# A layered kernel whose order is written out by hand: three constant products less, the modulation's first loads earlier, and all instructions listed anew

## The chip, the core and the metric

The kernel runs on one core of one Trainium2 chip. The core has a matrix engine (TensorE, PE in the profile, with its weight loads as PEld), a vector engine (VectorE, DVE), a scalar engine (ScalarE, ACT), a general one (GpSimd, POOL), and SyncE (SP), which here issues nearly all DMAs. Each engine works through its own instructions in order and waits on semaphores for the others. The metric is the device time of one execution in microseconds (us); lower is better. A time is the median of several runs.

## What is computed

Two token-mixing layers with adaptive normalisation, all in float32, on x of 2048 rows by 512 columns. The modulation vectors come from one row c:

```python
    x = A_x
    mod = (_silu(c) @ w_mod).reshape(c.shape[0], 6, 1, -1)
    sa, ca, ga, sb, cb, gb = (mod[:, 0], mod[:, 1], mod[:, 2], mod[:, 3], mod[:, 4], mod[:, 5])
    h = _layernorm(x, axis=-1) * (1 + ca) + sa
    x = x + ga * _A_ref(h, A_wqkv, A_w_phi, A_wo)
    h = _layernorm(x, axis=-1) * (1 + cb) + sb
    x = x + gb * _B_ref(h, B_w1, B_w2, B_w3, B_w4)
    return x
```

A is a linear attention with a learned feature map: there are 32 heads of 16 columns; keys and queries go through a small matrix per head, `w_phi`, and two softmaxes, and the sums go through wo. B is layernorm, w1, gelu, shifts along the rows and w2, then layernorm, w3, gelu and w4, with both halves added to their input; w1 and w2 are 512 by 512, w3 is 512 by 1376 and w4 is 1376 by 512.

## The kernel before

**Stages.** The rows are worked in 16 tiles of 128, two tiles making a chunk (8 chunks). First the per-head matrices are folded into the key and query weights on TensorE (`load_folded`, line 648: eight products of a loaded tile `rk` with a block-diagonal matrix `bd` that is made from a small constant and a mask). Then every chunk is normalised, turned by TensorE transposes, scaled and shifted by the modulation's columns (`h_chunk`, 685), and multiplied to keys, values and queries (`k_feat` 736, `q_feat` 764); the keys' features are summed with the values into one accumulator. Queries go to DRAM. The second stage (`phase_a`, 909) takes them back chunk by chunk, makes attention's output, wo, the second modulated norm, w1 and the shifts with w2. The last stage multiplies by w3 and w4 with a Strassen-like scheme of seven products for eight. The large weights and activations are split in a high part and a remainder (`hi_lo`), and three fast products of the parts stand for one product in full precision (`three`).

**The start.** `body` loads c and the identity from ScalarE's queue (`load_act`) and a small constant from SyncE's, fills a matrix `ones` on GpSimd, and issues nine constant products of `ones` with itself (lines 500 to 502), whose result nobody reads; each is four matmuls of 128 by 128 in float32, and each such matmul runs as two passes, so it makes eight records in the profile. `mod_cols` (529) makes the columns of sa and 1 + ca: silu of c (exp on ScalarE, then add, reciprocal and product on VectorE), a broadcast of it to `wide`, four loads `mod2` of 0.5 MB each, four groups of products of `wide` with them, a copy of the result out of PSUM, two transposes on TensorE and two small copies. The other four modulation vectors are made in full rows later, from sixteen more loads (`mod_acc`).

**What sets the order.** The program builds a list of operations first (class `Plan`, 283), numbers them as they are made, and then issues them in the order that the string `ORDER` gives (line 40, read in `order`, 352). A number may carry a letter that moves the operation to another engine it can run on (A for ScalarE, V for VectorE, G for GpSimd). Nothing else orders the work: one engine's queue is the subsequence of `ORDER` that falls to it. `SLOT` gives each tile the buffer it lies in, one character per tile; a tile whose buffer was in use waits for the last reader of the tile before. In SyncE's queue of before, the loads come in this order: four tiles of x, with the small constant after the second; two tiles `rk`; the four `mod2`; two `rk`; a tile of x; then the other four `rk` with a tile of x among them; then wv, x and the modulation's further loads. TensorE's queue begins with the nine constant products, one folded-weight product, four transposes of the first chunk, the four groups of modulation products, then more transposes (the third chunk's among them) and the other seven folded-weight products. ScalarE's queue begins with c's load, then a pass over a tile of x of the third chunk, and the identity's load behind that.

The mask and constant that make `bd` run on VectorE and GpSimd (`make_bd`, 641). Two layer norms are in use: one with its statistics on VectorE (`layernorm`, 572: the first chunk) and one on ScalarE (`layernorm2`, 612).

Of the kernel before, what the change touches and what calls it, by code (L numbers as in the profile page):

```python
# [164 lines left out]
)  # L165
SLOT = {
    "pp": "354206170301136260517505607442523070157475601660106031401453313745662015634523405103645651314210"
          "4326265450622670302462",
    "bd": "c3",
    "w": "124657de12834c6d075e18",  # L170
    "rk": "9768efjh",
# [1216 lines left out]
```

## Time and profile before

| | |
|---|---|
| median of 3 runs | 556.39 us (556.19 to 556.42) |
| the profiled execution | 556.38 us |
| its span, first to last instruction | 554.6 us |
| granted TensorE clock | 0.999 |
| DMA, mean over the span | 225 GB/s |
| moved by DMA | 124.90 MB |

How to read the rows of the profile: a line of the timeline has a start and a duration in us, the engine, the line of the code, the instruction, what it writes and reads by the program's names, and a count where several were merged; in brackets stands the idle time before it and who ended it. All matmuls have line 471, since one helper issues them, so groups are told apart by their names: `pp<-const` are the constant products, `pp<-mod,const` the modulation's, `pp<-bd,rk` the folded weights', `pp<-w,hh` keys, values and queries, `pp<-w,oT` wo, `pa<-nT,w` w1. A line of the windows has a stretch, its length, then per engine the busy time and the count, then the granted clock, the DMA's share and its GB/s. A line of the waits has who waited, for whom, the sum, how many times, and the longest.

### The profile page before, as it was taken

The page shows a single profiled execution, that of the slowest core. Times are in us where ns is not written, and L with a number is a line of the kernel's source. Part 1 is how long each engine was busy: PE and PEld are TensorE (multiplying, and loading weights), DVE is VectorE, ACT ScalarE, POOL GpSimd, SP SyncE. Part 2 cuts the span into 40 slices and gives each one's busy share as a digit, 9 for nine tenths or more (in the row PEclk, how much of TensorE's full clock was granted, in tenths as well). Part 3 has the DMA queues.
Part 4 walks back from the last instruction along what each step waited for, and adds up shares of the span by engine and source line. Part 5 has one row for each costly group of instructions (what it writes and reads, how often), then busy time and mean ns, then how long its engine had stood idle before and what let it go on. Part 6 is the DMA issues. An engine that isn't in the chain of part 4 may idle for free.

```text
span 554.6 us, 12399 instructions
## 1 busy us (share of the span) xinstructions
PE 548.3 (99%) x4522; PEld 491.5 (89%) x4522; DVE 484.6 (87%) x901; ACT 352.1 (63%) x833; POOL 339.5 (61%) x348
## 2 busy tenths in 40 slices
PE   9999999999999999999999999999999999999997
PEld 8888788888777788888889999999999999999996
DVE  3899997999999999999898788788788777888876
ACT  4789988644344788978888786867352535235540
POOL 3289849788799999986986533516334453133522
PEclk9999999999999999999999999999999999999999
DMA  8964651654765668687898888896976796572212
GB/s 317 386 215 148 212 161 42 214 173 143 247 193 158 221 212 232 238 294 256 269 298 267 274 297 276 281 324 250 382 232 241 264 379 204 174 249 93 59 58 76
DMA packets 63749, 124.90 MB, mean 225 GB/s; under 512 B 7140, under 2 KB 26852, under 8 KB 59592
## 3 DMA queue, kind: packets, MB, share of 16 engines
q1 hardware_dynamic: 63400, 124.04, 67.3%
q8 instruction: 35, 0.57, 0.4%
q14 instruction: 26, 0.21, 0.1%
q10 hardware_dynamic: 288, 0.07, 0.1%
HBM read 89.74 MB, written 34.35 MB: 224 GB/s over the span
## 4 chain that ended last, share of the span: by engine, by line
PE 61%; DVE 1%; DVEq 0%; issue 0%
PE pa L471 26%; PE ac L471 20%; PE pp L471 14%; PE pt L480 1%; DVE pT L762 0%; DVE pp L437 0%; DVE xb L418 0%; DVEq L1384 0%; DVEq L418 0%; DVEq L762 0%
## 5 line engine op out<-in xcount | busy, mean ns | idle before, releaser
L471 PE MATMUL pp<-w,hh 128*128 128x512 f32 x576 | 137.9, 396 | 0.0
L471 PEld LDWEIGHTS pp<-w,hh 128*128 128x128 f32 x576 | 106.8, 188 | 25.6 <-ACT qe L401 0.8
L471 PE MATMUL pa<-bH,wq 128*128 128x256 f32 x840 | 107.7, 281 | 0.0
L471 PE MATMUL ac<-w,gg 128*128 128x256 f32 x840 | 107.2, 281 | 0.0
L471 PEld LDWEIGHTS ac<-w,gg 128*128 128x128 f32 x840 | 103.6, 188 | 1.2
L471 PEld LDWEIGHTS pa<-bH,wq 128*128 128x128 f32 x840 | 103.7, 189 | 1.0
L471 PE MATMUL pp<-w,sh 128*128 128x512 f32 x192 | 50.1, 399 | 0.0
L471 PE MATMUL pa<-nT,w 128*128 128x256 f32 x384 | 47.8, 282 | 0.9 <-DVE nT L418 0.6
L471 PEld LDWEIGHTS pa<-nT,w 128*128 128x128 f32 x384 | 46.5, 188 | 2.4 <-DVE nT L418 1.1
L471 PE MATMUL pp<-w,oT 128*128 128x512 f32 x192 | 47.7, 396 | 0.0
L471 PEld LDWEIGHTS pp<-w,oT 128*128 128x128 f32 x192 | 35.5, 188 | 8.1 <-DVE oT L418 0.4
L420 POOL TENSOR_TENSOR gg<-cu,gg 128x128 fp32r<-128x128 f32 (+1 forms) x29 | 19.0, 667 | 38.1 <-PE ac L471 18.4
L471 PEld LDWEIGHTS pp<-w,sh 128*128 128x128 f32 x192 | 34.5, 188 | 7.7 <-issue 1.0
L401 ACT ACTIVATE cu<-pa 128x512 f32<-128x512 f32 (+1 forms) x39 | 20.1, 519 | 27.5 <-PE pa L471 21.3
L588 POOL TENSOR_TENSOR rs<-mv,const 128x2 f32<-128x2 f32 x31 | 22.6, 732 | 24.3 <-ACT mv L595 23.0
L401 ACT ACTIVATE gg<-cu 128x256 fp32r<-128x256 f32 (+1 forms) x64 | 21.2, 357 | 23.7 <-PE ac L471 17.4
L420 POOL TENSOR_TENSOR e<-e,q 128x1024 f32<-128x1024 f32 x16 | 31.2, 1966 | 1.2 <-DVE q L418 1.1
L420 POOL TENSOR_TENSOR ez<-e,const 128x1024 f32<-128x1024 f32 x12 | 29.8, 2490 | 2.8 <-ACT const L401 2.8
L401 ACT ACTIVATE gg<-sg 128x512 fp32r<-128x512 f32 x37 | 22.5, 623 | 13.5 <-POOL sg L420 8.2
L418 DVE TENSOR_TENSOR gg<-sg,gg 128x512 fp32r<-128x512 f32 x38 | 26.8, 707 | 4.6 <-ACT gg L401 3.3
L401 ACT ACTIVATE cu<-cu 128x512 f32<-128x512 f32 (+1 forms) x36 | 19.3, 550 | 12.0 <-DVE cu L418 12.0
L418 DVE TENSOR_TENSOR cu<-pa,cu 128x512 f32<-128x512 f32 (+1 forms) x36 | 21.1, 593 | 6.4 <-PE pa L471 5.3
(214 smaller groups left out, 1212.4 us busy)
## 6 DMA issues: line engine op xcount, KB each, us to landing
wq<-dram SPq DMA_DIRECT2D x32, 1024.0 KB, 6.8
dram<-ws SPq DMA_DIRECT2D x35, 256.0 KB, 3.0
xl<-in_x SPq DMA_DIRECT2D x32, 256.0 KB, 4.3
dram<-qe SPq DMA_DIRECT2D x16, 512.0 KB, 2.9
e<-dram SPq DMA_DIRECT2D x64, 128.0 KB, 3.6
raw<-in_w SPq DMA_DIRECT2D x18, 256.0 KB, 3.9
mod<-in_wmod SPq DMA_DIRECT2D x16, 256.0 KB, 5.3
dram<-xl SPq DMA_DIRECT2D x16, 256.0 KB, 3.4
```

Of the source, the lines that this page charges most:

```text
L401: nc.scalar.activation(o(), i(), func, **kw)
L418: dve = ("DVE", 71 + 1.04 * o.n + 90 * (isps(a) and isps(b)), lambda: nc.vector.tensor_tensor(o(), a(), b(), op=op))
L420: pool = ("Pool", cost, lambda: nc.gpsimd.tensor_tensor(o(), a(), b(), op=op))
L471: nc.tensor.matmul(o(), a(), b(), start=s, stop=e, **kw)
L480: nc.tensor.transpose(o(), i(), ident())
L588: plan.op("Pool", 540 + 10 * m, lambda: nc.gpsimd.tensor_tensor(r(), v(), mhalf[:, :m](), op=OP.pow), [r], [v, mhalf])
```

## The change

Three things change. The constant products are six in place of nine; all operations made after them have numbers lower by three. `ORDER` is written anew in full, and `SLOT` with it. And a few operations go to other engines: counted by the letters and the engines that operations have without one, 340 of the 2801 operations that both kernels share run on another engine than before (103 from GpSimd to VectorE, 101 from VectorE to GpSimd, 58 from VectorE to ScalarE, 53 back, 16 from ScalarE to GpSimd, 9 back). What each operation computes stays.

```diff
 ORDER = (
-    "0 3 45 12 38 2 240 10 46 7 47 48 87 13 49 242 239 30 26 53 57 55 39 59 34 40 1 41 4 22 241 42 43 6 50 243 "
+    "1 10 3 42 0 4 35 2 50 54 5 52 56 23 36 31 9 11 88 85G 43 27 37 44 12 86 45 8 19 18 13 14 15 49G 38 39 51 100 "
+    "6 46 40 16G 7 41V 237 17 47 53 87 48G 55 57 62 58V 92 236 59 24 96 60 84 61 63V 67 81 25 32 68V 64 679 69 89 "
...
 SLOT = {
...
-    "rk": "9768efjh",
+    "rk": "72634eg9",
-    "xl": "10di5208hfgb4cf0ea0c4kd9f3ihj36146gb9b9508ikhj73",
+    "xl": "10ikfbdb9h23j8l640adjlk9g876e46lfdil3j080678278h",
...
     plan.at("warm")
-    for _ in range(9):
+    for _ in range(6):
         p = T("pp", [P, NK, P])
         mms([(p[:, k, :], ones, ones, True, True) for k in range(NK)], [p], [ones])
```

Read back from the two strings, the queues begin like this after the change.

- SyncE: two tiles of x, the small constant, the four `mod2` (first, third, second, fourth), six tiles `rk`, a tile of x of the third chunk, `rk`, the other such tile, `rk`, then wv's first tile, the second chunk's x and so on.
- TensorE: four constant products, the first group of modulation products, the other two constant products, the three further groups of modulation products, four transposes of the first chunk, the two transposes of the modulation's columns, a folded-weight product, the other four transposes of the first chunk, the seven other folded-weight products, then two key products and a query product of the first chunk, the second chunk's transposes, a query product, the third chunk's transposes.
- ScalarE: the identity's load, c's load, the exp of silu, then copies of the folded weights and of the first chunk; the third chunk's norm after these.
- VectorE: both first statistics, silu's steps with masks among them, a norm of the first chunk, then the modulation's copies and the split of the first chunk and of the folded weights.
- GpSimd: `ones`, a mask, the broadcast to `wide` (on ScalarE before), the first two reciprocal roots.

More of the change, by code (lines that the diff above doesn't have):

```diff
@@ L40 @@
 ORDER = (
[124 rows of a table removed]
[124 rows of a table added]
 )
 SLOT = {
[L167 to L170, printed above, removed]
-    "rk": "9768efjh",
-    "xl": "10di5208hfgb4cf0ea0c4kd9f3ihj36146gb9b9508ikhj73",
-    "st": "40d3i38fc51di08ac4jah174d1ga5f06d",
-    "mv": "51fa026ig6bf351di08i8dg27dei6e59b",
-    "rs": "62gb497302ag46bf35236be1i703938ai",
-    "nm": "78eh9cj51badh4ej897chej297ghe69cj29c08bgbf45fhjach42j17g",
@@ L177 @@
-    "xn": "gbaba47ai968db2j",
-    "mod": "l6l76g452h91di45e2",
+    "pp": "015632614340517032150643012526242367251411661166312763426267553575313027152161025567307111272635"
+          "0055072172642262056",
+    "bd": "85",
+    "w": "125634cd180254b6d83c72",
+    "rk": "72634eg9",
+    "xl": "10ikfbdb9h23j8l640adjlk9g876e46lfdil3j080678278h",
+    "st": "01b8h659g68cf15bdj7928gdc6g92if59",
+    "mv": "23fa07aej79eh68cf18f6bh7gbie5123a",
+    "rs": "54gd18ci13agj79eh2305a13e4jfb07ce",
+    "nm": "67ci9ej23b4dfh025b4di023a4gi05cd73ci06ahaeh14j894jd68bgh",
@@ L179 @@
+    "xn": "ac6e20j076ibfkic",
+    "mod": "dja8441l7ei4agf6ga",
     "mod2": "0213",
-    "kva": "2",
+    "kva": "0",
     "za": "6",
-    "hh": "0839abc0",
-    "pt": "25327461613743570652324305736521",
-    "raw": "c21k18h7715djgf362a0fhae27gf",
-    "k1": "1045013501501501",
-    "ke": "5489712089712354",
-    "k2": "5234231243234323",
-    "vv": "a7dk85gac5hbb21h",
-    "qe": "6720487161942819",
-    "q1": "2330454052043312",
-    "qt": "kkbhb78bg11b",
-    "acc": "j3lcg",
-    "kvs": "2",
@@ L194 @@
-    "pz": "7",
-    "q2": "03123513",
-    "e": "0983705304169074",
-    "ez": "2320522197506115",
-    "q3": "1245045014204250",
-    "q5": "15504152",
-    "pT": "4528179545810889",
-    "oT": "6a6ca009",
-    "nT": "b0766b9a",
-    "n": "g7dh24k4bj74g816",
-    "h": "5j7ge851ckdij4c5",
-    "gf": "27586896",
-    "sh": "95b9ae91",
-    "pa": "641235350522652635114703427320411671025643770736145372603453",
-    "wr": "35632",
-    "ws": "l6d9h3a4820k5c8chb8h2d2k7920b8f8c3d",
-    "gb": "l",
-    "tw": "54235",
@@ L212 @@
-    "bL": "17827583",
-    "nb": "979h32306d3ae5k9",
-    "yt": "3dg52b83k86hjehh",
-    "bH": "06946142097189309001918205215851",
-    "tr": "b3bj5235i0j1e29j",
-    "wq": "075e2ab923b9a23ba9b32ba932ba23ab9a32",
-    "cu": "910bdi843kjc02akf9bhe35j061ig2h41eg8b7cj",
-    "gl": "h48h9962",
-    "ac": "16455436740134572306167215764032",
-    "gg": "73961754365316475286104928316462703941562370961249647091642708964235190243756189",
-    "sg": "kec291637e7die18bdch9cakf7g3cdi602di3cj4",
-    "xb": "fg6g5d74b8fakf59",
@@ L224 @@
-    "xc": "6a134j6g8h22dh30",
-    "uu": "a3ee5c1d",
+    "hh": "0789abe7",
+    "pt": "72547173634774753001231627404702",
+    "raw": "9c3h5d79b2kfiche513a9hifgjl2",
+    "k1": "0114230103143431",
+    "ke": "4529730459817324",
+    "k2": "0451352502052531",
+    "vv": "h0ec840g7d05bh2b",
+    "qe": "7601181576971729",
+    "q1": "3252402454123154",
+    "qt": "2c30khikc02k",
+    "acc": "5kf1a",
+    "kvs": "2",
+    "pz": "4",
+    "q2": "03125315",
+    "e": "0953845341605891",
+    "ez": "3622216688880646",
@@ new lines @@
+    "q3": "1245043014204230",
+    "q5": "00032504",
+    "pT": "7466688584766450",
+    "oT": "96b3a9a6",
+    "nT": "a94baace",
+    "n": "6hh66h6hl5861454",
+    "h": "cia4ej0ckg72de3c",
+    "gf": "29470579",
+    "sh": "7e67edc7",
+    "pa": "371003132710576017436532106014275314360517374703257106341757",
+    "wr": "82032",
+    "ws": "d231ghe76gjgk921dff1b2haci9k6k1k55l",
+    "gb": "b",
+    "tw": "79265",
+    "bL": "81374028",
+    "nb": "895d50a15424dg12",
+    "yt": "7fd13408i9df3723",
@@ L226 @@
+    "bH": "64478207159823612653094704091721",
+    "tr": "k96hada5ikcl1hkl",
+    "wq": "739391ae09ae109e109ae091ea010e1a09e1",
+    "cu": "a10ki95f8j0jh81a6e4kk2l9d4g06ecj3f51k80l",
+    "gl": "lifhc6dj",
+    "ac": "45722570314275103624062315204736",
+    "gg": "95426980426801459802938176385986135927068341579637175369405638749056132790864257",
+    "sg": "hee3ae4ddlg325dd07ic8h71hik879h7d29l7h42",
+    "xb": "6cc7g43jf5gei0a9",
+    "xc": "g4lg29lh522ihglc",
+    "uu": "li7al636",
 }
```

245 rows, old and new, of the table ORDER are left out of this document.

## The prediction

> **What bounds the kernel now.** I read the page first: the engines' totals, then the chain that ended last.
>
> ```profile
> span 554.6 us, 12399 instructions
> PE 548.3 (99%) x4522; PEld 491.5 (89%) x4522; DVE 484.6 (87%) x901; ACT 352.1 (63%) x833; POOL 339.5 (61%) x348
> PE 61%; DVE 1%; DVEq 0%; issue 0%
> ```
>
> TensorE is busy for 548.3 of 554.6 us, and the chain is almost all matmuls from 211 us to the end. So the time is TensorE's work, plus what it loses at the start, at stalls, and after its last matmul. The profiled execution took 556.38 us, 1.8 us more than its span; the median of the three runs is 556.39, so sums made against this profile need no shift. The rows below are TensorE's own timeline at the start, then pieces of it cut out by two narrower windows, then the end.
>
> ```profile
> 0.98 11.09 PE L471 MATMUL pp<-const 128*128 128x128 f32 x72 [0.98 <-POOL const L498]
> 11.90 1.06 PE L471 MATMUL pp<-bd,rk 128*128 128x128 f32 x8
> 13.56 1.93 PE L471 MATMUL pp<-mod,const 128*32 128x256 f32 x32
> 15.43 1.09 PE L480 MATMUL pt<-const,xn 128*128 128x128 f32 x8
> 17.02 6.42 PE L471 MATMUL pp<-bd,rk 128*128 128x128 f32 x56
> 23.19 5.86 PE L471 MATMUL pp<-w,hh 128*128 128x512 f32 x24
> 0.98 5.70 PE L471 MATMUL pp<-const 128*128 128x128 f32 x25 [0.98 <-POOL const L498]
> 6.99 4.85 PE L471 MATMUL pp<-const 128*128 128x128 f32 x42
> 550.22 0.52 PE L471 MATMUL ac<-w,gg 128*128 128x256 f32 x3
> 550.85 0.75 DVE L418 TENSOR_TENSOR xb<-xb,ac 128x256 f32<-128x256 f32 x2 [0.86 <-PE ac L471]
> ```
>
> The nine constant products are the 72 records of the first row (4 matmuls of two passes each). They come at two rates: 25 in 5.70 us, one per 0.213 us, and from about 6.7 us on 42 in 4.85 us, one per 0.112. Real work starts at 11.90 and then TensorE hardly stops. After that start its waits on other engines are these three, 1.2 us in all, where the first chunks' normalised tiles (nT, n) are awaited, between 186 and 206 us:
>
> ```profile
> PE pa L471 <- DVE nT L418: 0.6, 2, 0.3
> PE pt L480 <- ACT n L401: 0.3, 1, 0.3
> PE pa L471 <- ACT nT L401: 0.3, 1, 0.3
> ```
>
> The second reading is VectorE's, by stages (busy time, then counts):
>
> ```profile
> 0.00:23.19 23.19, 12.54 (x34) 1.00 0.95 345
> 23.19:80.00 56.81, 55.38 (x79) 1.00 0.61 196
> 80.00:100.00 20.00, 16.92 (x26) 1.00 0.31 104
> 100.00:190.25 90.25, 88.00 (x127) 1.00 0.63 195
> ```
>
> And all engines' further on (PE, PEld, DVE, ACT, POOL, each busy time and count):
>
> ```profile
> 190.25:260.00 69.75, 69.08 (x639) 59.26 (x640) 67.99 (x118) 57.57 (x136) 60.45 (x57) 1.00 0.73 236
> 260.00:354.00 94.00, 94.00 (x733) 84.98 (x732) 80.64 (x149) 74.82 (x187) 57.94 (x69) 1.00 0.83 278
> 354.00:550.85 196.85, 196.74 (x1616) 194.30 (x1614) 162.39 (x373) 92.69 (x224) 72.47 (x111) 1.00 0.64 219
> ```
>
> 190.25 us is where the first w1 products start. From 23 us to there VectorE is busy for 160 of 167 us: it is a second limit just behind TensorE, and only its early work has room.
>
> **The constant products.** Three products of 8 records go. The 25 slow records stay, because the four products still at the head hold 32; what goes is 24 records at 0.112 = **2.7 us**. They are on the path: TensorE is busy from 0.98 on. But they also covered the wait for the first loads, so the question is what is late next.
>
> **The loads.** SyncE issues in order. Before, the modulation's four loads of half a megabyte stand behind four tiles of x, the small constants and two of the folded weights; now they stand behind two tiles of x and the constants. Rates and landings:
>
> ```profile
> 0.00:3.00 3.00, 2.02 (x9) 2.03 (x10) 0.00 (x0) 1.28 (x1) 0.39 (x5) 1.00 0.33 100
> 3.00:6.00 3.00, 3.00 (x16) 3.00 (x15) 2.20 (x8) 0.00 (x0) 0.57 (x1) 1.00 1.03 346
> 6.00:9.00 3.00, 3.00 (x26) 3.00 (x25) 0.61 (x4) 2.62 (x8) 1.76 (x3) 1.00 1.04 372
> 9.00:12.00 3.00, 3.00 (x29) 3.00 (x28) 1.63 (x7) 2.22 (x8) 1.60 (x3) 1.00 1.02 398
> 3.99 2.65 SPq L448 DMA_DIRECT2D mod<-in_wmod x4
> mod<-in_wmod SPq DMA_DIRECT2D x1, 512.0 KB, 5.8
> mod<-in_wmod SPq DMA_DIRECT2D x1, 512.0 KB, 7.5
> ```
>
> The last column of the windows is GB/s, so 0.30 MB had moved by 3 us, 1.34 by 6, 2.45 by 9, 3.65 by 12. The first modulation load landed at 3.99 + 5.8 = 9.8; with all ahead of it, it is byte 2.23 million, moved by 8.4: 1.4 us from the last byte to the landing. The third (issued 4.94, 7.5) gives the same 1.4. The queue is never empty, so the new order goes by bytes. The first load ends at 1.25 MB (the identity, now issued first on ScalarE at 0.72 in place of 6.32, is in it): moved by 5.7, landed 7.1. The third (needed second) ends at 2.29 MB: landed 9.95. The last ends at 2.82 MB: landed **11.3**, where before it was the byte 3.80 million, about 13.8. The folded weights' tiles follow, one per 0.7 us from 11.9; TensorE takes one per 0.9 us from 12.7, so they hide. What is moved back behind them, the two tiles of x for the third chunk and ScalarE's work on them, is next needed at 32 us; it hides too.
>
> **The silu of c.** The modulation's stationary operand needs c through exp, add, reciprocal, product, and a broadcast. Before it was ready at 12.0, because ScalarE had its work behind a wait for x. These rows price it:
>
> ```profile
> 3.56 0.69 DVE L574 BATCH_NORM_STATS2 st<-xl 128x6 f32<-128x512 f32 x1 [3.56 <-DMA xl<-in_x]
> const<-in_c ACTq DMA_DIRECT2D x1, 2.0 KB, 3.0
> 6.32 0.63 ACT L401 ACTIVATE xn<-xl 128x512 f32<-128x512 f32 x1 [3.87 <-DMA xl<-in_x]
> 9.58 0.19 ACT L401 ACTIVATE const<-const 128x4 f32<-128x4 f32 x1
> 10.29 0.17 DVE L445 RECIPROCAL const<-const 128x4 f32<-128x4 f32 x1
> 11.72 0.29 ACT L401 ACTIVATE const<-const 128x128 f32<-128x128 f32 x1
> 12.71 0.45 POOL L420 TENSOR_TENSOR bd<-const 128x128 f32<-128x128 f32 x1
> ```
>
> Now c's load goes second on ScalarE, about 0.4 later, and lands at 4.1 with nothing of x ahead of it. VectorE does two statistics first (the second tile of x, one tile's 0.26 MB behind the first at the rate of the 3 to 6 us row, lands at about 4.4; then 2 x 0.69), five small ones at 0.15 to 0.2 and two masks at 0.25 among them: the product is done at about 7.3. The broadcast goes to GpSimd, of which no such row exists: at least ScalarE's 0.29, at most the mask's 0.45. I take 0.4: ready at 7.7. Both ends differ by 0.2 us.
>
> **TensorE's new start, step by step.** Four constant products end at 7.4. First modulation product at 7.7 (idle 0.3), 1.93/4 = 0.45 long with its gap. Two constant products, 16 x 0.112 = 1.8, to 9.95, as the next load lands. Two modulation products to 10.85. The last load lands at 11.3 (idle 0.45); product to 11.75, drained 11.9. Four transposes of x fit behind it. Then the queue holds two transposes of the evicted sums in front of everything: they need VectorE's eviction,
>
> ```profile
> 15.57 0.42 DVE L410 TENSOR_SCALAR mod<-pp 128x256 f32<-128x256 f32 x1 [1.16 <-PE pp L471]
> ```
>
> so they start at 11.9 + 0.1 + 0.42 + 0.1 = 12.5 (idle 0.3) and end at 12.7. Eight folded-weight products (64 x 0.112 = 7.2) and four transposes (0.45) follow without a wait: the first key product starts at **20.3**. Before it started at 23.19, with 0.9 us of the third chunk's transposes (two groups of four) already done that now come later: 22.3. The lead is **2.0 us**, of the 2.7; the other 0.7 went into the new waits.
>
> [...]
>
> **Behind it, up to 30 us.** VectorE has 38 instructions listed ahead of the first key reduction, 14 of them 512 wide at 0.6 to 0.69 us, by rows about 15 us; it can start the bulk of them when the columns are there, at 13.3 (12.7 and an eviction) where the row below has 17.05, and the reduction can't start before 23.2.
>
> ```profile
> 17.05 1.59 DVE L410 TENSOR_SCALAR pt<-pt,const 128x256 f32<-128x256 f32 x3
> ```
>
> So it arrives with 15 us done where before it had 12.54 by then. The next tight place is the second chunk's first transposes at 20.3 + 8.5 = 28.8 (three products, 5.86/2 each less the overlap): one of their tiles is now normalised on VectorE, behind the second key product's first reduction, at 28.6 to 29.5. I count 0.2 us. SyncE's later loads wait for buffers as before.
>
> **The order anew.** 340 of 2801 instructions change engines, but the work of each engine stays within 3 us (VectorE +1, ScalarE -2, GpSimd +3, at the durations of before's groups). TensorE's list keeps its shape: ahead of the first w1 products stands the same work less the constants, and between the first chunk's output projection and its transposes the same filler (two num groups, two query products, three quarter projections). So the stalls there remain. VectorE's list ahead of those products trades 28 instructions (15.1 us) for 31 (17.8; 1.59/3 for the 256 wide, 0.6 to 0.69 for the 512, 1.2 for the 1024): 172.85 + 2.7 = 175.6 us. Its idle time before was 10.65 us up to 23.19, and 6.75 after. With 2.5 less at the start (15 done for 12.54): 8.1. Were the later 6.75 unchanged, the products would start at 175.6 + 8.1 + 6.75 = 190.4; without the 3.1 of 80 to 100 us, when VectorE had run ahead and waited for TensorE, at 187.3. TensorE itself gets there at 190.25 - 2.0 + 0.2 = 188.5. I take 188.7. From 354 us on VectorE has 34 us of room. The last group is the same: final matmuls, two additions of 0.4 us, two stores. Cost nothing; what would cost is the broadcast addition on GpSimd just ahead, done 0.8 us early by my count.
>
> **Sum:** -2.7 + 0.7 + 0.2 + 0.2 = **-1.6 us: 554.8**.
>
> **Rivals.**
> *The stalls go too.* VectorE reaches 190 us ahead of TensorE (187.3), so part of the 1.2 us of stalls and some switching loss vanishes: 553.8 down to 552.4. Against it: the wait for nT is a chain of transpose, copy and difference behind one quarter projection, the same in both lists.
> *VectorE takes it back.* If its idle time after 23 us is what it was, the first w1 products start at 190.4 and the end stays: 556.4, between 555.3 and 557.5. For it speaks that 2.7 us were added to its list; against it, that the 3.1 us were waiting for TensorE.
> *Slower, by VectorE's queue.* The same place: each us beyond counts fully, because behind 190 us TensorE has no idle time to give. It decides at 7.8 us of idle time after 23 us (start at 191.5, 1.2 us late); at 10, VectorE having waited for ScalarE and GpSimd inside its own order, it is 193.7 and 559.8. Nothing in the lists shows such waits, but an order anew has them somewhere.
> *Slower, cold.* If the modulation's loads landed as late as before (13.8), TensorE would sit idle from 10.85, 3 us in place of 0.45, which turns the 1.6 us gained into 0.9 lost: 557.3, or, if the slow rate came back for 5.7 us as in the row of 25, 2.7 more: 560.0. The bytes speak against it. [...]
>
> **How the numbers follow.** The forecast (553.8 to 555.3) has 0.46, the stalls' rival 0.14, VectorE taking it back 0.20, slower by its queue 0.13, cold 0.07. About 0.2%, 1.1 us, is what a measurement here can tell from no change: faster 0.60, same 0.20, slower 0.20. The range leaves out the ends of both sides: 552.4 to 558.4.
>
> **What would show it.** Right: 48 constant records, the first four modulation products between 7.7 and 12, key products from 20.3; TensorE waiting three times under half a us; w1's first products near 188.7; the end 3.8 us after the last matmul. Wrong: a wait above 1 us in the first 13 us (loads or silu), a TensorE wait at 29 us for the second chunk's tile, a first w1 product after 190, or new stalls in the last stage, for which I have no row.

## The result, and the profile after

The changed kernel takes **558.45 us** (median of 6 runs, 557.63 to 559.66) against 556.28 us (6 runs) of the kernel before: ratio 1.0036, 95% interval 1.0024 to 1.0049. It is slower, by 2 us, where I forecast 1.6 us faster. Beside the last experiments it was timed once more: 557.96 us in 12 runs, ratio 1.0027 (1.0014 to 1.0040). The profiled execution took 557.92 us with a span of 556.1, 1.5 us more than before's 554.6. The page has these lines for it: the span, the engines' totals, the chain by engine.

```profile
span 556.1 us, 12353 instructions
PE 545.4 (98%) x4498; PEld 488.6 (88%) x4498; DVE 487.7 (88%) x898; ACT 350.1 (63%) x831; POOL 345.1 (62%) x353
PE 86%; DVE 7%; DMA 3%; POOL 2%; issue 1%; DVEq 0%; ACT 0%; POOLq 0%
```

TensorE is busy 2.9 us less than before (545.4 against 548.3), near the 2.7 us of the forecast, and yet the span is longer. The chain tells where to look: VectorE holds 7% of it, where it held 1%.

TensorE's own waits, in the changed kernel (who, on what, total, times, longest):

```profile
PE pp L471 <- ACT kvs L401: 1.5, 1, 1.5
PE pp L471 <- DMA mod<-in_wmod: 1.4, 3, 1.0
PE pp L471 <- DVE pT L762: 1.1, 1, 1.1
```

The first and the last are new and long: a wait for `kvs` (the copy of the keys' and values' sums) and one for `pT` (a transposed tile of the first query group). Before, neither product waited at all. First the start, from TensorE's timeline of the changed kernel:

```profile
0.97 5.72 PE L471 MATMUL pp<-const 128*128 128x128 f32 x32 [0.97 <-POOL const L498]
7.70 0.64 PE L471 MATMUL pp<-mod,const 128*32 128x256 f32 x8 [1.01 <-DMA mod<-in_wmod]
...
10.54 1.07 PE L471 MATMUL pp<-mod,const 128*32 128x256 f32 x16 [0.23 <-DMA mod<-in_wmod]
...
20.79 8.53 PE L471 MATMUL pp<-w,hh 128*128 128x512 f32 x36
```

The start does what was forecast: first modulation product at 7.70, key products from 20.79 (forecast 20.3). Now the same two products in both timelines, the changed kernel first, then the kernel before. A row is a run of merged matmuls: a query product, which covers the time until `kvs` is copied, then the product with `kvs` (group kvb), behind another query product the one with `pT` (group num0).

```profile
154.57 3.04 PE L471 MATMUL pp<-w,hh 128*128 128x512 f32 x12
159.09 0.66 PE L471 MATMUL pp<-const,kvs 128*64 128x128 f32 x8 [1.48 <-ACT kvs L401]
...
163.86 1.16 PE L471 MATMUL pp<-pT,const 64*32 64x128 f32 x64 [1.14 <-DVE pT L762]
```

```profile
156.21 3.05 PE L471 MATMUL pp<-w,hh 128*128 128x512 f32 x12
159.19 0.67 PE L471 MATMUL pp<-const,kvs 128*64 128x128 f32 x8
...
162.76 1.16 PE L471 MATMUL pp<-pT,const 64*32 64x128 f32 x64
```

At the query product ahead of kvb the changed kernel is 156.21 - 154.57 = **1.64 us ahead**, which is the whole forecast gain. Nine microseconds later it is 163.86 - 162.76 = **1.10 us behind**: 1.48 + 1.14 us of waits. So this loss is made in one place. What stood still there shows in the queues behind the two waits; VectorE first, then GpSimd, then ScalarE, all of the changed kernel:

```profile
140.93 1.85 DVE L418 TENSOR_TENSOR ke<-ke,k 128x1024 f32<-128x1024 f32 x1
142.70 1.21 DVE L418 TENSOR_TENSOR qe<-qt,q 128x1024 f32<-128x1024 f32 x1
143.83 0.68 DVE L418 TENSOR_TENSOR w<-raw,w 128x512 fp32r<-128x512 f32 x1
144.74 1.23 DVE L418 TENSOR_TENSOR ez<-e,const 128x1024 f32<-128x1024 f32 x1 [0.23 <-ACT const L401]
145.88 2.63 DVE L418 TENSOR_TENSOR ws<-ws 128x256 fp32r<-128x256 f32 x1
148.43 1.78 DVE L418 TENSOR_TENSOR w<-raw,w 128x512 fp32r<-128x512 f32 x1
...
153.66 1.27 DVE L442 TENSOR_REDUCE q<-qt 128x32 f32<-128x512 f32 x2
```

```profile
139.28 2.41 POOL L420 TENSOR_TENSOR za<-za,ke 128x1024 f32<-128x1024 f32 x1
145.78 2.45 POOL L420 TENSOR_TENSOR ez<-e,const 128x1024 f32<-128x1024 f32 x1 [4.09 <-ACT qe L401]
148.19 1.47 POOL L420 TENSOR_TENSOR w<-raw,w 128x512 fp32r<-128x512 f32 x1
155.07 2.03 POOL L420 TENSOR_TENSOR qe<-qt,q 128x1024 f32<-128x1024 f32 x1 [5.41 <-DVE pz L437]
```

```profile
157.13 1.15 ACT L401 ACTIVATE qe<-qe 128x512 f32<-128x512 f32 x2 [5.15 <-POOL qe L420]
...
158.66 0.37 ACT L401 ACTIVATE kvs<-kva 128x256 f32<-128x256 f32 x1
```

Compare like with like on VectorE. The operation on `w` takes 0.68 at 143.83 and 1.78 at 148.43; the one on 1024 columns takes 1.21 at 142.70 and 1.85 at 140.93; the 256 wide one on `ws` takes 2.63, where the group of its kind has a median of 0.415:

```profile
L418 DVE TENSOR_TENSOR ws<-ws x9: 408/415/2628, 77.8 to 315.9; 128x256 fp32r<-128x256 f32 x9
```

That is 1.10 + 0.64 + 2.21 = 3.95 us. Each of the three begins while GpSimd runs an operation and ends only after it: `ws` at 148.51, GpSimd's `ez` at 145.78 + 2.45 = 148.23. Such time counts as busy here (2.63 us in the row of `ws`), so VectorE looks full. All of these operations, on both engines, read two tiles from SBUF. And the delay travels by the queues. The reductions of query group q8 (of q0 to q15) end at 154.9 (153.66 + 1.27); GpSimd, idle for 5.41 us, subtracts their result (`qe`) until 157.10; ScalarE's two exponentials and a `qt` stand behind that and ahead of `kvs`, which is copied at 158.66, though TensorE had gone on from `kva`'s sums to the query product at 154.57.

### The profile page after: what moved, and what is told of

Same layout as the page of the kernel before. It is cut to its first block, busy times and chain, and to the rows that moved or that the text cites. A ratio compares the mean times of both kernels' runs of the same rounds, so it can differ in the third digit from the quotient of the medians.

```text
span 556.1 us, 12353 instructions
## 1 busy us (share of the span) xinstructions
PE 545.4 (98%) x4498; PEld 488.6 (88%) x4498; DVE 487.7 (88%) x898; ACT 350.1 (63%) x831; POOL 345.1 (62%) x353
## 4 chain that ended last, share of the span: by engine, by line
PE 86%; DVE 7%; DMA 3%; POOL 2%; issue 1%; DVEq 0%; ACT 0%; POOLq 0%
PE pp L471 36%; PE pa L471 27%; PE ac L471 20%; PE pt L480 2%; DVE pz L442 1%; DMA mod<-in_wmod 1%; DVE q L442 1%; PE kva L471 1%; POOL qe L420 1%; DVE pT L762 1%; DMA wr<-in_w 1%; POOL e L420 1%; DMA const<-in_id 1%; DVE ws L418 0%; DVE ez L418 0%
## 5 line engine op out<-in xcount | busy, mean ns | idle before, releaser
L420 POOL TENSOR_TENSOR gg<-cu,gg 128x128 fp32r<-128x128 f32 (+1 forms) x28 | 17.5, 633 | 36.4 <-PE ac L471 11.3
L401 ACT ACTIVATE gg<-cu 128x128 fp32r<-128x128 f32 (+1 forms) x64 | 21.3, 354 | 18.7 <-PE ac L471 11.0
L420 POOL TENSOR_TENSOR w<-raw,w 128x512 fp32r<-128x512 f32 (+3 forms) x16 | 19.6, 1229 | 20.5 <-DVE w L410 12.0
L418 DVE TENSOR_TENSOR gg<-sg,gg 128x512 fp32r<-128x512 f32 x36 | 25.3, 706 | 7.8 <-PE pa L471 3.9
L420 POOL TENSOR_TENSOR ke<-ke,k 128x1024 f32<-128x1024 f32 x14 | 27.1, 1942 | 0.0
```

The source lines that it names most:

```text
L401: nc.scalar.activation(o(), i(), func, **kw)
L418: dve = ("DVE", 71 + 1.04 * o.n + 90 * (isps(a) and isps(b)), lambda: nc.vector.tensor_tensor(o(), a(), b(), op=op))
L420: pool = ("Pool", cost, lambda: nc.gpsimd.tensor_tensor(o(), a(), b(), op=op))
```

## The experiments

Three theories. **Turns**: VectorE's two-input operations stand still while GpSimd runs one, in turns, and the queues carry that to kvb and num0. **Length**: VectorE simply has more work listed ahead of num0. In both lists each operation taken at its median, that is about 160.6 us against 154.0 up to the transposition that num0 waits for, 6.6 us more (the expectations say 5); the forecast had looked further down, at w1's first products, and found 2.7. **Place of kvs**: `kvs` stands behind the exponentials in ScalarE's queue, and that alone is the loss. The rivals of the start are tried as well. Numbers in `ORDER` are the changed kernel's: 784 is the operation on `ws`, 672 the remainder on `w.11` (a subtraction; the expectations call it a product), 708 and 706 the two `ez`, 709 the reduction of the first, 460 the last q8 reduction, 680 `kvs`, 669 GpSimd's remainder.

**e1: the operations spread.** Three words of VectorE's list are moved, nothing else.

```diff
-    "508 579 639 888 578 889 671 539 890 454 521 571 541G 661 572 640 580 630 473 659 675G 641 475 885 581 538 "
+    "508 579 639 888 578 889 784 671 539 890 454 521 571 541G 661 572 640 580 630 473 659 675G 641 475 885 581 538 "
...
-    "653G 294 380 705 295 648 584 647 381 683 649 684 903 663 603 685 605 382 708 652 383 457 731 784 384 672 785 "
-    "706 799G 709 650 458 707 459 669G 460 465 797 651 710 461G 711 712 713 714 796 717G 463 654 800 462 587 466 "
+    "653G 294 380 705 295 648 584 647 381 683 649 684 903 663 603 685 605 382 708 709 652 383 457 731 384 785 "
+    "706 799G 650 458 707 459 669G 460 672 465 797 651 710 461G 711 712 713 714 796 717G 463 654 800 462 587 466 "
```

> The changed kernel with three words of VectorE's list moved: the addition on ws.3 to about 120 us, where GpSimd is idle, the reduction of ez.1 directly behind ez.1, the product on w.11 behind the reductions of the 8th query group. Same operations, same engines, the same set ahead of num0. Theory 'turns' (VectorE's two-input operations on SBUF tiles stand still while GpSimd runs one: 0.63 + 2.21 + 1.09 us lost at 140.9 to 150.2 us of the changed kernel): the last q8 reduction ends near 152.0 instead of 154.9, TensorE's waits ahead of kvb (1.48) and num0 (1.14) go, and the end comes 2.0 to 2.9 us earlier: 555.6 to 556.5 us, ratio to before 0.998 to 1.001. Theory 'length' (VectorE's list ahead of num0 is 5 us longer, whatever its order): both waits stay, 558.2 to 558.7 us. Theory 'place of kvs' (kvs stands behind the q8 exponentials in ScalarE's queue): kvb's wait shrinks no more than these exponentials come earlier, num0's stays; 557.5 to 558.4 us.

Measured: **555.04 us** (554.61 to 558.19, 6 runs), ratio 0.9983 (0.9965 to 1.0001), 2.9 to 3.4 us less than the changed kernel's medians and somewhat more than expected. VectorE of e1, then its GpSimd, then TensorE:

```profile
145.44 1.23 DVE L442 TENSOR_REDUCE pz<-ez 128x64 f32<-128x1024 f32 x1
146.57 2.17 DVE L418 TENSOR_TENSOR ez<-e,const 128x1024 f32<-128x1024 f32 x1
...
149.91 1.27 DVE L442 TENSOR_REDUCE q<-qt 128x32 f32<-128x512 f32 x2
151.10 0.68 DVE L418 TENSOR_TENSOR w<-raw,w 128x512 fp32r<-128x512 f32 x1
```

```profile
145.21 2.44 POOL L420 TENSOR_TENSOR ez<-e,const 128x1024 f32<-128x1024 f32 x1 [4.10 <-ACT qe L401]
```

```profile
156.97 0.67 PE L471 MATMUL pp<-const,kvs 128*64 128x128 f32 x8
...
160.72 1.16 PE L471 MATMUL pp<-pT,const 64*32 64x128 f32 x64
```

With the same operations on the same engines, the q8 reductions end at 151.2 in place of 154.9, kvb's wait is gone and num0's nearly so. The reduction at 145.44 also shows what did not collide here: it has one input, runs wholly opposite GpSimd's `ez`, and takes its usual 1.23. Of the stalls, 0.96 us is left on `ez` and 0.6 on `ke`. Length alone fails here: the set ahead of num0 is the same (ahead of the q8 reductions, and so of kvb, it is one operation of 0.68 us shorter). But the longer list and TensorE's lead had used up the room. Before, num0's last operand was ready at 161.70 (161.29 + 0.41 on VectorE) and TensorE came at 162.82; in e1 the operand is ready at 160.67 (159.43 + 1.24) and TensorE comes at 160.62. Any stall on top of that is a wait. Of the 3.3 us between the two profiled executions (557.92 and 554.66), 0.57 was there ahead of all this, at the query product (154.00 against 154.57), from a shorter start.

**e2: kvs ahead of the exponentials.**

```diff
-    "706 799G 709 650 458 707 459 669G 460 465 797 651 710 461G 711 712 713 714 796 717G 463 654 800 462 587 466 "
-    "464 680 887 467 715G 718 798 801G 681 588 522 468 682 716 469G 802 984 719 523 589 907G 720 1482 803 530 524 "
+    "706 799G 709 650 458 707 459 669G 460 465 797 651 710 461G 711 712 713 714 796 717G 463 654 800 680 462 587 466 "
+    "464 887 467 715G 718 798 801G 681 588 522 468 682 716 469G 802 984 719 523 589 907G 720 1482 803 530 524 "
```

> The changed kernel with kvs (the copy of kva.0 for the kvb product) moved ahead of the two q8 exponentials and of qt.5 in ScalarE's queue, nothing else. Theory 'place of kvs': kvb's wait of 1.48 us goes, and 1.5 us or more comes back at the end: 556.9 us or less. Theories 'turns' and 'length': kvb's wait goes, but num0 waits for pT.0, which ends as late as before (163.8 us), so num0's wait grows from 1.14 to 2.5 us and the end stays: 558.2 to 558.7 us.

Measured: 558.23 us (557.96 to 559.33, 5 runs), ratio 1.0034 (1.0022 to 1.0046): no gain. Its TensorE:

```profile
158.43 0.67 PE L471 MATMUL pp<-const,kvs 128*64 128x128 f32 x8 [0.48 <-ACT kvs L401]
...
164.49 1.29 PE L471 MATMUL pp<-pT,const 64*32 64x128 f32 x64 [2.42 <-DVE pT L762]
165.70 4.45 PE L471 MATMUL pp<-w,hh 128*128 128x512 f32 x12
```

kvb's wait shrinks by 1.0 us and num0's grows by 1.3: in both kernels the same transposition on VectorE ends num0's wait. The place of `kvs` is a link, not the cause. In the last row twelve records take 4.45 us in place of 3.04; that comes back below.

**e8: one word of e1 alone** (784, as in e1's first line pair, and taken out of its old place).

> The changed kernel with only one of e1's three words moved: the addition on ws.3, which stood still for 2.21 us opposite GpSimd's ez.2, goes to about 120 us, where GpSimd is idle. If that stall belongs to this operation, 2.2 us come back on VectorE and with it most of kvb's and num0's waits: 556.0 to 556.6 us. If the two engines take turns at whatever stands next in VectorE's queue, the product on w.11 now stands still in its place until GpSimd's ez.2 ends (near 148.2 us), ez.0 behind it until GpSimd's product on w.11 ends, and only the addition's own 0.4 us comes back: the waits stay above 2 us in sum, 557.6 to 558.4 us.

Measured: 557.53 us (556.81 to 559.36, 12 runs), ratio 1.0020 (1.0007 to 1.0034), 0.4 us less than the changed kernel beside it. Its VectorE, then its GpSimd:

```profile
145.84 2.89 DVE L418 TENSOR_TENSOR w<-raw,w 128x512 fp32r<-128x512 f32 x1
148.66 2.31 DVE L418 TENSOR_TENSOR ez<-e,const 128x1024 f32<-128x1024 f32 x1
```

```profile
145.74 2.44 POOL L420 TENSOR_TENSOR ez<-e,const 128x1024 f32<-128x1024 f32 x1 [4.10 <-ACT qe L401]
148.15 1.74 POOL L420 TENSOR_TENSOR w<-raw,w 128x512 fp32r<-128x512 f32 x1
```

The stall does not go with the operation. What stands next now waits for GpSimd's `ez` (0.68 becomes 2.89), and `ez` behind it for GpSimd's remainder (1.21 becomes 2.31). The two engines take turns here: the four operations end at 148.18 (GpSimd), 148.73, 149.89 (GpSimd) and 150.97.

**e5: the same collision put into the kernel before.** One word is moved by one place on VectorE; there 675 is the remainder, 709 `ez`, with 688 the scale that it needs.

```diff
-    "382 588 650G 390 798 389 391 865 890 384 686 589 606 393 687 660 386 608 675 688 460 392 709 665 394 652 "
+    "382 588 650G 390 798 389 391 865 890 384 686 589 606 393 687 660 386 608 688 460 392 709 675 665 394 652 "
```

> The kernel before with one word of VectorE's list moved by one place: the product on w.11 (0.69 us, needed only at 212 us) stands behind ez.0 in place of ahead of it, so that it meets GpSimd's ez.1. Same operations, same engines, the same set ahead of kvb and num0. Theory 'turns': ez.0 still starts at 147.0 (it waits for the scale of z), VectorE loses 0.6 us ahead of it, GpSimd takes its turn at 148.2, the product then lasts until 150.5 to 151.2 (about 3 us in place of 0.69), the q8 reductions end near 153.5 in place of 151.7, num0's product waits 0.5 to 1.2 us for pT.0, and the end comes 0.8 to 1.6 us later: 557.2 to 558.0 us, ratio 1.0015 to 1.003. Theory 'length' (only what stands ahead counts): nothing changes, 556.2 to 556.6 us.

Measured: **557.95 us** (557.48 to 558.43, 6 runs), ratio 1.0031 (1.0020 to 1.0043). Its VectorE, GpSimd and TensorE:

```profile
147.01 1.22 DVE L418 TENSOR_TENSOR ez<-e,const 128x1024 f32<-128x1024 f32 x1 [0.52 <-ACT const L401]
148.15 2.90 DVE L418 TENSOR_TENSOR w<-raw,w 128x512 fp32r<-128x512 f32 x1
```

```profile
147.06 3.45 POOL L420 TENSOR_TENSOR ez<-e,const 128x1024 f32<-128x1024 f32 x1 [2.47 <-ACT const L401]
```

```profile
163.39 1.16 PE L471 MATMUL pp<-pT,const 64*32 64x128 f32 x64 [0.53 <-DVE const L418]
```

One word that nobody waits for until 212 us, moved by one place, costs 1.5 us in an otherwise untouched kernel, about the price of the whole change. Its profile is 0.6 us behind at num0 (163.39 against 162.76) and 1.6 behind at w1's first product (191.86 against 190.25), with a further wait of 0.63 us for `oT` between the two; the delay on VectorE meets more than one product. First GpSimd waits (its `ez` takes 3.45 in place of 2.44, ending 2.3 us after VectorE's), then VectorE does (2.90 in place of 0.68).

**e3: nine constant products again**, in the changed kernel; the numbers from 10 on rise by three.

```diff
-    for _ in range(6):
+    for _ in range(9):
```

> The changed kernel with nine constant products again (three more behind the last of the six, ahead of the first modulation product), all else as changed. If VectorE's list is full and sets kvb and num0 whatever TensorE does before ('length', no slack): the start's 1.6 us lead is simply not there to lose, first modulation product near 9.8 us, kvb's and num0's waits shrink by what the start loses, end within 0.5 us of the changed kernel: 558.2 to 558.9 us. Theory 'turns' (the stall sits at a fixed place of the order and moves with everything else): the start loses 1.6 to 2.4 us and the waits stay at 1.3 to 1.5 and 1.1, end 560.0 to 560.8 us.

Measured: 559.17 us (558.69 to 559.48, 5 runs), ratio 1.0047 (1.0035 to 1.0059). The first modulation product starts at 9.87, and the waits stay as they were:

```profile
160.55 0.67 PE L471 MATMUL pp<-const,kvs 128*64 128x128 f32 x8 [1.48 <-ACT kvs L401]
...
165.33 1.16 PE L471 MATMUL pp<-pT,const 64*32 64x128 f32 x64 [1.14 <-DVE pT L762]
```

The stall moves with everything else, as turns expect: VectorE is not so full that an earlier start would only wait longer. The cost by profiles is 1.5 us (559.42 against 557.92), by medians 0.7 to 1.2, less than the 1.6 to 2.4 expected, so that the time lies between the two theories' ranges.

**e4 and e7: six constant products alone**, in the kernel before; the same kernel twice. The edit is that of the change, `range(9)` to `range(6)`, with before's order.

> The kernel before with six constant products in place of nine and nothing else: loads and order as before. If the constant products themselves held the start: 24 x 0.112 = 2.7 us earlier, 553.7 us. If the first transposes wait for the identity and the first modulation products for their loads anyway (before: 13.0 us): TensorE idles where the three products stood, first transpose at 13.0 as before, end within 0.4 us of before: 555.9 to 556.6 us.

> The kernel before with six constant products again, for a profile of one of its longer runs: its five timed runs took 557.7 to 560.0 us at a mean granted clock of 0.994 to 0.997, its profiled one 556.7 at 0.998. If the idle time in the start (0.66 and 1.74 us) lowers the granted clock soon after it, the profile shows a stretch below 1.00 within the first 40 us and the same lists behind it; if the time is lost elsewhere, the clock falls at another place.

Measured: 558.16 us (556.68 to 560.03, 6 runs), ratio 1.0033 (1.0016 to 1.0049), and 557.82 in the single run of e7: slower, against all I expected. e4's profiled execution was the shortest of its six, 556.68 us; e7's took 557.82. TensorE of e7, then two of its windows (busy time and count of TensorE; the third number from the end is the granted clock):

```profile
10.08 1.16 PE L471 MATMUL pp<-bd,rk 128*128 128x128 f32 x8 [1.25 <-DVE bd L418]
12.84 1.09 PE L480 MATMUL pt<-const,xn 128*128 128x128 f32 x4 [1.60 <-DMA const<-in_id]
13.86 2.94 PE L471 MATMUL pp<-mod,const 128*32 128x256 f32 x32
```

```profile
9.12:12.54 3.42, 1.16 (x8) 1.00 1.01 401
12.54:15.95 3.41, 3.11 (x24) 0.50 1.03 394
```

With three products less, TensorE waits for a mask and then for the identity, and after 1.25 and 1.60 us of idling the granted clock is 0.50 for 3.41 us: the 32 modulation records take 2.94 us, 1.93 before. So the constant products that nobody reads had a use there. The other longer runs had no profile, so that they lost their time in the same way is not shown; their mean granted clock was 0.994 to 0.997, where e4's profiled run had 0.998.

**e6: two more waits, meant to go.** e1, and the reductions of two later groups' `ez` (910, 1015; the expectation calls them an addition and a statistic) moved behind an operation of num1 and one of n0 that TensorE waits for.

```diff
-    "694 909G 904 737 738 739 811 740 729 741 744 1012 813 1005G 742 595 816 690G 745 814 743 695 1480 910 746 "
-    "748 666G 747 815 911 696 819 749 692 750 912 817 691 1014G 913 752 825 693 1011 751 757 1119 753 914 820 697 "
-    "985G 1001 915 1015 916G 758 754 759 826 821 755 760 822 1002G 756 823 918G 827 730 1003 917 765 830 831 1006 "
+    "694 909G 904 737 738 739 811 740 729 741 744 1012 813 1005G 742 595 816 690G 745 814 743 695 1480 746 "
+    "748 666G 747 815 910 911 696 819 749 692 750 912 817 691 1014G 913 752 825 693 1011 751 757 1119 753 914 820 697 "
+    "985G 1001 915 916G 758 754 759 826 821 755 760 822 1002G 756 1015 823 918G 827 730 1003 917 765 830 831 1006 "
```

> The spread kernel (e1) and two more swaps in VectorE's and ScalarE's lists, meant for the two waits that are left at 180 to 188 us, oT and nT: the next group's addition moved behind the operation of o2 that stood after it, and one statistic of a later tile behind that of n0. If these two waits (0.2 and 0.8 us in e1) are the queues' order, they go and the end comes 0.5 to 0.9 us before e1: 554.1 to 554.6 us, ratio to before 0.996 to 0.9975. If VectorE is simply full there, 555.0 as e1.

Measured: **555.26 us** (554.12 to 555.99, 11 runs), ratio 0.9978 (0.9968 to 0.9987): faster than both kernels. The waits for oT and nT are gone, but a new one of 0.63 us stands at 190.87, again for `pT`, and the median is e1's within their scatter. The gain of these two words is not shown.

**e9: e6 with nine constant products**, and **e10: the changed kernel once more.**

> The best order (e6) with nine constant products in place of six, all else as there: what the start is worth once nothing behind it waits. The first modulation product starts near 9.9 in place of 7.3 to 8.4 us; TensorE then has no wait for the loads, first key product near 22.2. By the start's timelines (e3 against the changed kernel: 1.46 us at the 12th query group) the end comes 1.4 to 2.2 us after e6: 556.6 to 557.4 us. If VectorE's list and not TensorE sets the end, less than 0.5 us after e6: 555.3 to 555.8 us.

> The changed kernel as it is, beside e8 and e9 on one chip, since its six runs lay between 557.6 and 559.7 us: 557.9 to 558.9 us again. If one of its two long waits lowers TensorE's granted clock in some runs, as e2's wait of 2.4 us did, a profile with a stretch below 1.00 right behind 159 or 164 us would show it, near 559.5 us.

Measured: e9 555.94 us (555.71 to 556.56, 12 runs), ratio 0.9993 (0.9981 to 1.0005); e10 557.96 (557.03 to 559.24, 12 runs). e9 falls between its two expectations: against e6 three constant products cost 0.7 us of the median, or 0.8 by the ratios (0.9993 and 0.9978, whose intervals just overlap).

With nine constant products the first modulation product waits for nothing (it starts at 9.19 us in e9, at 9.87 in e3). With six it starts between 7.3 and 8.4 us in the six profiles of such kernels that I have, after 1.0 to 1.9 us of idling. The twelve runs of e9 lie within 0.9 us, those of the kernels with six 1.4 to 3.6 us apart; but the kernel before, which has nine, spread over 4.1 us in 29 runs beside e9, so that the products make the times steadier is not shown. The fastest run of e6 is also its profiled one (554.12), so the profiles put e6 1.7 us ahead of e9 (555.86) where the medians have 0.7. e10's profile shows no lowered clock at its waits of 1.5 and 1.1 us.

## Why the prediction was wrong

**The start: right in its times.** First modulation product 7.70 (forecast 7.7), three waits of 0.2 to 1.0 us, key products at 20.79 (20.3). That the 7.7 came out is in part luck: the broadcast was ready at 7.30 (7.00 + 0.30 on GpSimd) and not at 7.7, and the product waited for its load, which I had landed at 7.1. The idle time ahead of the first product was 1.0 in place of 0.3, because the four constant products ended at 6.69 and not 7.4: all 32 records took 5.72 us, where I had taken the rate to change after 25. The 1.64 us of lead at 154.57 is the forecast 1.6.

**The order anew: this step failed**, in two of its sentences. "VectorE's list ahead of those products trades 28 instructions (15.1 us) for 31": I priced each operation by its group's usual duration and weighed the list at one place, w1's first products. Three of them lasted 3.95 us longer than that, opposite GpSimd. And "the stalls there remain", "nothing in the lists shows such waits": the lists, laid side by side, did show two-input operations of both engines opposite each other. The kernel before even has the sign, in GpSimd's row:

```profile
147.03 5.82 POOL L420 TENSOR_TENSOR ez<-e,const 128x1024 f32<-128x1024 f32 x2 [2.78 <-ACT const L401]
```

Two operations take 5.82 us there, where one alone takes 2.44; the other 0.9 us is a wait behind VectorE's `ez`. The prediction made nothing of it. In the rivals' terms it is "slower by VectorE's queue", which I gave 0.13. It was placed at w1's first products with the price of idle time; it came 30 us earlier, as busy time, and by way of GpSimd's and ScalarE's queues.

**The sum.** In the profiles: 1.64 us gained at the start, 2.74 lost by num0, 0.9 regained by w1's first products (190.45 against 190.25, so 0.20 behind; before's products had waited between), then 1.3 lost to the end. Of this last part 0.8 us lies between w1's first products and the last matmul, 0.4 of it in that first group itself and the rest in many small differences of pace. The other 0.5 is the tail, 4.36 us after the last matmul in place of 3.83. One of the last product's four records is missing in both traces, so the tail's part may be the trace's. No run tried these two, and they stay open.

**Taking it back and cold.** "VectorE takes it back" had w1's first products at 190.4, and they are at 190.45, with VectorE busy for 175.7 us up to there, as it had counted (175.6). That is a coincidence: 3.95 us of it is standing still, and e1, with the same operations on VectorE up to there, reaches w1's first product at 187.12, about where the prediction had it without waits (187.3). It also had the end follow from there at 556.4, and 1.3 us more came behind. "Cold" didn't happen in the profiled run: behind its waits of 1.01, 0.23 and 0.21 us in the start the granted clock stayed at 1.00. The 560.0 took a slow rate that comes back for 5.7 us after a wait, which no run shows; the lowered stretches of e2 and e7 lasted 3.41 us each. That idling in the start can lower the clock is shown by e7, for another kernel; whether it is in the changed kernel's longer runs is open.

## What to carry to other kernels

An engine's list isn't priced by its own durations alone: three operations of VectorE took 3.95 us longer here opposite GpSimd's. Lay the lists of the two beside each other, and look for a pair of two-input operations at the same time, above all two long ones next to short ones (in e5 the short one behind such a pair took 2.90 us in place of 0.68). Give the one that waits a one-input neighbour there (in e1 a reduction, which took its usual 1.23 us opposite GpSimd's `ez`): with this and two more words moved, all on VectorE, e1 took 2.9 to 3.4 us less. A time won at the start is worth what the next tight queue lets through, so check it at the first product that waits for a long chain across engines, not at the one that waited before.

## What the runs showed of the hardware

- **Turns.** In e8, where VectorE and GpSimd both had two-input operations queued, they alternated, one each: its four operations above end in turn, at 148.18 (GpSimd), 148.73, 149.89 (GpSimd) and 150.97. VectorE, which waits there, is shown as busy: `w` begins at 145.84, when the operation before it ends, and takes 2.89 us in place of 0.68. Not every such pair waits: in the changed kernel the 128 wide operation on `q` and `pz` at 155.10 takes 0.29 us opposite GpSimd's `qe` (155.07 to 157.10), and the eight of its kind take 0.27 to 0.29.
- **The clock after short idling.** In e2, behind an idle time of 2.42 us, the granted clock was 0.50 for 3.41 us, and the 12 records of one product took 4.45 us for 3.04. The granted clock changes at 6.84 and 552.97 us in the kernel before, 160 times 3.413 us apart, and at 4.94 and 554.49 us in the changed kernel, 161 times; the two lowered stretches inside a kernel (e2 and e7) last one such step. The rows show the step ahead of the drop and the lowered one in e2, then in e4 the place at which e7 lost its clock and e4 kept it:

```profile
161.97:165.38 3.41, 0.99 (x65) 1.00 0.00 0
165.38:168.79 3.41, 3.41 (x26) 0.50 0.77 217
10.09:13.50 3.41, 1.67 (x16) 1.00 1.02 401
13.50:16.91 3.41, 3.41 (x47) 1.00 1.05 395
```

  TensorE was idle for 71% of the step in e2 and 66% in e7 (1.16 busy of 3.42, above), and for 51% in e4, where one of the two idle times fell into the step before. Behind the last matmul the clock falls to 0.50 after a step that was idle for 65% before, for 80% in the changed kernel and for 51% in e4. In before and the changed kernel no earlier step brought a drop; the most idle of them, 161.95 to 165.37 us of the changed kernel, was idle for 33%. So whether one kernel loses its clock can hang on where the steps fall in that run; a border finer than "about half" is not shown.
- **The slow first period** is neither a fixed time nor a fixed number of records in these traces. The first entry of the trace's clock (the windows read 1.00 ahead of it for want of one) stands at 6.84 us before, 4.94 after and 4.12 in e1, 5.9, 4.0 and 3.1 us behind the first matmul; about there the pace goes from one record per 0.213 us to one per 0.112. So 25 records took 5.70 us before, 32 took 5.72 after, and the first 32 took 5.33 in e1.
